# A recurrent attention kernel with a fused SwiGLU block: two more units have their k and r turned by DMAs inside SBUF and VectorE, and the last store is split

## The chip, the cores and the metric

The kernel runs on one core of a Trainium2 chip. The metric is the device time of one execution in microseconds (us), the median of several runs. Lower is better. The engines are named as in the profile: PE is TensorE (PEld its weight loads), DVE is VectorE, ACT is ScalarE, POOL is GpSimd, SP is SyncE, which here only issues DMAs. "SPq" and "ACTq" stand for the DMA issues of SP and ACT.

## What is computed

An RWKV5 attention (4 batches, 8 heads, 768 tokens, head width 48) feeds a SwiGLU feed-forward block with 3072 tokens, model width 384 and inner width 1536. All is float32.

```python
for t in range(S):
    cur = np.einsum('bhd,bhe->bhde', u[None] * kt, vt)
    y[:, :, t] = np.einsum('bhd,bhde->bhe', rt, state + cur)
    state = w[None, :, :, None] * state + np.einsum('bhd,bhe->bhde', kt, vt)
...
g = x @ w_gate
silu = g * (1.0 / (1.0 + np.exp(-g)))
val = x @ w_val
return (silu * val @ w_out).astype(np.float32)
```

## The kernel before

**Units and stages.** The tokens of a batch are cut into six chunks of 128. A unit is one chunk of one batch; there are 24, and unit i is chunk i // 4 of batch i % 4. The function `fast` does the work. (A second function, `general`, only runs when a decay lies outside a range; it does not run here.) The order on every engine is the order of the program text. Units 0 to 3 are written out by hand, then a loop runs over stages s = 4 to 25. Stage s scales k and r of unit s+1 on POOL (`scale`, L299 and L302) and forms its products r·k·u (`own_product`, L228 and L229), loads v of unit s+1 and k and r of unit s+3 (`load_v` L121, `load` L115, both on SP's queue), brings k and r of unit s into transposed form, forms the score matrix of unit s-1 (`scores`, PE at L379, DVE at L384), and computes the outputs of unit s-2 (`outputs`, L409) and its state update (`update`, PE at L424, DVE at L436, POOL at L437).

**Two ways to transpose k and r.** The scaled k and r of the units lie in one tile, `hats`, which has four places for k and two for r. For units below `BLOCKS` (12 before) the function `turn` does 8 PE transposes into two PSUM banks (L341, tile `tp`), and ACT copies both banks to the tiles `kT` and `rT` (L345). From `BLOCKS` on, `move_blocks` issues 16 DMAs on SP's queue (L356, shown as hats<-hats), which arrange 32x32 blocks of one unit's k and r into two spare places of `hats`, and `turn_blocks` has DVE transpose within the blocks, one instruction for `kT` and one for `rT` (L371). The two spare places exist once: `move_blocks` of unit i+1 waits for `turn_blocks` of unit i. In stage s the loop calls `turn_blocks(s)` and then `move_blocks(s + 1)`, behind the scores of unit s-1.

**Places for r.** Below `BLOCKS`, r of unit i lies in place i % 2. From `BLOCKS` on, two consecutive units share a place: `i % 4 // 2`. So units 12 and 13 use one place, 14 and 15 the other. `scale_r` of the second unit of such a pair writes where `move_blocks` of the first reads.

**Feed-forward work.** Groups of 256 tokens (two units) go through gate and value products. `gate_value` (L448) does groups 0 and 1 straight: six matrix products into one of two PSUM banks of the tag `gv`, a sigmoid on ACT (L454), and two products on DVE (L455 and L456) that write `hT`. Later groups, two at a time, go through a scheme with fewer products (`four`, L625). The output projection of two groups is a sequence of items, each of six products into PSUM (`project`, L519). An item "gi" below means item i of the projection, with g the group: 0 or 1 of the pair. The items come in this order:

```python
order = "00 10 01 02 11 04 03 12 05 06 13 14 15 16".split()
```

where the first digit is the group and the second the item. Item 0 of a group takes a bank of the tag `gv` for one of its accumulators; in group 0 that bank is used by item 1. Item 10 and item 01 call `h_sums`, two wide additions each on DVE (L492 to L496), ahead of their matrix products. POOL forms sums of weights (`weight_sum`, L476) that the projections need.

**What fills a stage.** In stages 5 to 11 the table `EARLY` says where a weight is rounded or summed ("R") and where one piece of feed-forward work is fed ("F"). In stages 9 to 11 an F stands behind the scores, another behind outputs and update, and a third at the end of the stage. The piece behind the update in stage 11 is the last gate and value product of group 1; the piece at the stage's end is item 00; items 10, 01 and 02 open the feeding of stage 12.

**The outputs.** ACT issues the DMAs that store the result (L542). For the last pair of groups the tile of the first half of the tokens, `o_sb1`, is filled in two halves by DVE: columns 0 to 191 at item 1 (L529), columns 192 to 383 at item 6 (L533), the last computing instruction of the program. The whole tile is stored after item 6.

Of the kernel before, what the change touches and what calls it, by code (L numbers as in the profile page):

```python
# [15 lines left out]
P = 128  # L16
# [6 lines left out]
def fast(  # L23
# [31 lines left out]
    N = B * NCH  # L55
    DM, DFF = moe_w_gate.shape
# [11 lines left out]
    dve, pool, act, pe, sp = nc.vector, nc.gpsimd, nc.scalar, nc.tensor, nc.sync  # L68
# [26 lines left out]
    khat, rhat = [hats[:, n] for n in (0, 2, 3, 5)], [hats[:, n] for n in (1, 4)]  # L95
# [4 lines left out]
    blocks = [hats[:, n].rearrange("p h x -> p (h x)") for n in (7, 6)]  # L100

    def rhat_of(i):
        return rhat[i % 2 if i < BLOCKS else i % 4 // 2]

    def raw(i):

# [4 lines left out]
    def load(i):  # L111
        c, b = divmod(i, B)
        rows = slice(P * c, P * (c + 1))
        for src, dst in zip((k, r), raw(i)):
            sp.dma_start(out=dst, in_=src[b, :, rows, :].rearrange("h t d -> t h d"))  # L115

    def load_v(i):
        c, b = divmod(i, B)
        rows = slice(P * c, P * (c + 1))
        for e in range(2):  # L120
            sp.dma_start(  # L121
                out=v_ld[i % 4][:, :, 64 * e : 64 * e + D],
                in_=v[b, :, rows, :].rearrange("(a e) t d -> e t a d", e=2)[e],
            )
# [3 lines left out]
    for f in range(FC // 2):  # L128
        for src, dst in ((moe_w_gate, wg), (moe_w_val, wv)):
            cols = slice(2 * P * f, 2 * P * (f + 1))  # L130
# [94 lines left out]
    def own_product(i):  # L225
        kl, rl = raw(i)
        rk = two.tile([P, H, D], FP32, name="rk", tag="rk")[:]
        pool.tensor_mul(rk, rl, kl)  # L228
        pool.tensor_mul(rk, rk, ub[:])  # L229
        rks[i] = rk  # L230

    def own_sum(i):
        dus[i] = three.tile([P, H], FP32, name="du", tag="du")
        dve.tensor_reduce(dus[i][:], rks.pop(i), axis=AX.X, op=ALU.add)
# [9 lines left out]
    for e in range(2):  # L244
# [3 lines left out]
        out=ub[:].rearrange("p h d -> p (h d)"),  # L248
        in_=bass.AP(tensor=u.tensor, offset=u.offset, ap=[[0, P], [1, H * D]]),
# [9 lines left out]
    def warm(n):  # L259
# [9 lines left out]
        out=mask[:], in_=mask[:], compare_op=ALU.is_gt, fill=0.0,  # L269
# [7 lines left out]
    for l in range(7):  # L277
        n = 1 << l
# [15 lines left out]
    def at(i, a):  # L294

        return HP - 1 - a if i >= BLOCKS and i % 2 == 0 else a

# [3 lines left out]
    def scale_r(i):  # L301
        pool.tensor_mul(rhat_of(i)[:, :, 0:D], raw(i)[1], rscale[:])  # L302
# [8 lines left out]
    def scale(i):  # L311
        scale_k(i)
        scale_r(i)
# [18 lines left out]
    def pair(t, a):  # L332
        return t[:, 2 * a : 2 * a + 2, :].rearrange("p e d -> p (e d)")

    def turn(i):
        kr = khat[i % 4], rhat_of(i)
        tps = [ps_a.tile([P, HP, P], FP32, name="tp", tag="a") for _ in kr]
        turned[i] = three.tile([P, HP, P], FP32, name="rT", tag="rT")
        for tp, t, dst, table in zip(tps, kr, (kT[i % 2], turned[i]), (pw[:, :, 1 : P + 1], pv)):
            for a in range(HP):  # L340
                pe.transpose(tp[:, a, :], pair(t, a), ident[:])  # L341
            if i < 4:
                dve.tensor_mul(dst[:], tp[:], table)
            else:
                act.copy(dst[:], tp[:])  # L345
# [21 lines left out]
    def turn_blocks(i):  # L367

        turned[i] = three.tile([P, HP, P], FP32, name="rT", tag="rT")
        for dst, src in ((kT[i % 2], blocks[0]), (turned[i], blocks[1])):  # L370
            dve.transpose(dst[:].rearrange("p a t -> p (a t)"), src)  # L371

    def scores(i):

        ps = [ps_a.tile([P, HP, P], FP32, name="s_ps", tag="a") for _ in range(2)]
        for a in range(HP):
            for e in range(2):
                rows = slice(64 * e, 64 * e + D)
                pe.matmul(  # L379
                    ps[e][:, a, :], kT[i % 2][rows, at(i, a), :], turned[i][rows, at(i, a), :],  # L380
                    start=True, stop=True, skip_group_check=True,
                )
        for e in range(2):
            dve.copy_predicated(  # L384
                At[i % 2][:].rearrange("p (a e) t -> p a e t", e=2)[:, :, e],
                mask[:].bitcast(INT32).unsqueeze(1).to_broadcast([P, HP, P]), ps[e][:],
            )
# [77 lines left out]
    FH, NH = FC // 2, DM // 2  # L465
# [15 lines left out]
    def h_quarters(g):  # L481
        return [
            hT[g][:, FH * k : FH * (k + 1), P * j : P * (j + 1)] for j in range(2) for k in range(2)
        ]
# [13 lines left out]
    def project(g, n):  # L498

        h11, h12, h21, h22 = h_quarters(g)  # L500
        x = part_of.setdefault(g, {})
        if n == 0:
            one_bank = ps_f.tile([P, 2, 2 * P], FP32, name="o_f", tag="gv")[:, 0, 0:NH]
            if g % 2 == 0:
                x["a"] = ps_o.tile([P, 2 * P], FP32, name="o_a", tag="o")[:, 0:NH]
                x["b"] = one_bank
            else:
                x["a"] = one_bank
                x["b"] = ps_w.tile([P, 2 * P], FP32, name="o_b", tag="w_mag")[:, 0:NH]
            x["out"] = [two.tile([P, DM], FP32, name=n, tag=n) for n in ("o_sb1", "o_sb2")]  # L510
        lhs, rhs, acc = (
            (h11, w11, "a"), (h12, w21, "b"), (1, wt[0], "a"), (2, wt[1], "a"),
            (0, w12, "b"), (h22, wt[2], "a"), (3, w22, "b"),
        )[n]
        if isinstance(lhs, int):
            lhs = x["s"][lhs]
        ps = x[acc]
        for f in range(FH):
            pe.matmul(  # L519
                ps, lhs[:, f, :], rhs[:, f, :],  # L520
                start=(f == 0 and n in (0, 1, 4)), stop=(f == FH - 1), skip_group_check=True,
            )
        o1, o2 = x["out"]
        if n in (0, 2, 3):
            nm = {0: "p1", 2: "u2", 3: "u3"}[n]
            x[nm] = six.tile([P, 2 * P], FP32, name=nm, tag="part")[:, 0:NH]
            act.copy(x[nm], ps)
        elif n == 1:
            dve.tensor_add(o1[:, 0:NH], x["p1"], ps)  # L529
        elif n == 5:  # L530
            act.copy(o2[:, 0:NH], ps)
        elif n == 6:
            dve.tensor_add(o1[:, NH:DM], x["u2"], ps)  # L533
        if n in (3, 4):
            if "c22" in x:
                dve.tensor_add(o2[:, NH:DM], x["u3"], x["b"])
            x["c22"] = True
        if n >= 5:
            j = 6 - n
            c, b = divmod(2 * g + j, B)  # L540
            n0 = S * b + P * c
            act.dma_start(out=out[n0 : n0 + P, :], in_=x["out"][j][:])  # L542

# [155 lines left out]
    def gaps(s, n):  # L701

        if s not in EARLY:
            if n == 0:
                share[0] = min(-(-len(todo) // (4 - (s - 9) % 4)), 14)
            feed(share[0] // 5 + (n < share[0] % 5))
            return
        for what in EARLY[s][n]:
            if what == "R":
                if done["pool"] < NW:  # L710
                    round_weights()
                elif len(summed) < 4:
                    weight_sum()
            else:
                feed(1, 3)

    share = [0]
    BLOCKS = 12
    LATE = 12
    EARLY = {s: ("" if s < 7 else "R", "F", "R", "F", "RF") for s in range(5, 12)}  # L720
    EARLY[4] = ("R", "F", "", "F", "F")
# [82 lines left out]
    for s in range(4, N + 2):  # L804
        if 4 < s < N:
            own_sum(s)
        if s + 1 < N:
            scale(s + 1)
            own_product(s + 1)
            load_v(s + 1)  # L810
            if s + 3 < N:
                load(s + 3)
        if s < BLOCKS:
            turn(s)
        gaps(s, 0)
        if 4 <= s - 1 < N:
            while small:
                small.popleft()()
            scores(s - 1)
            if s >= LATE:  # L820
                outputs(s - 2)
                update(s - 2)
            gaps(s, 1)
        if BLOCKS <= s < N:
            turn_blocks(s)
        if BLOCKS <= s + 1 < N:
            move_blocks(s + 1)
        gaps(s, 2)
        if s - 2 >= 4 and (s < LATE or s > N):
            outputs(s - 2)  # L830
            update(s - 2)
        if s >= 5 and s % 2:
            queue((s - 3) // 2)
        if s < N:
            diagonal(s)
        if s - 2 >= 4:
            gaps(s, 3)
        gaps(s, 4)
        if s == 12:

            dve.tensor_tensor(bad[:], held[:], wcol[:], ALU.not_equal)
            dve.tensor_reduce(badc[:], bad[:], axis=AX.X, op=ALU.add)
            dve.memset(ones[:], 1.0)
            n_ps = ps_a.tile([P, HP, P], FP32, name="n_ps", tag="a")
            pe.matmul(n_ps[0:1, 0, 0:1], badc[:], ones[:], start=True, stop=True)
            act.copy(outside, n_ps[0:1, 0, 0:1])
# [417 lines left out]
```

## Time and profile before

| | |
|---|---|
| median of 5 runs | 625.47 us (624.91 to 628.15) |
| the profiled execution | 625.54 us, its span 623.7 us |
| PE busy | 611.1 us, 98% of the span |
| POOL busy | 296.9 us, 48% |
| DVE busy | 359.1 us, 58% |
| ACT busy | 238.8 us, 38% |
| PE transposes, tile tp | 96 of them, the last group at 113.96 us |
| hats<-hats DMAs | 192, from 119.73 us on |
| last computing instruction | DVE L533, 618.30 to 618.65 us |

The trace records one execution. Its span is the time from the first to the last record, and the execution's own time is 1.84 us longer. Busy shares are means over the whole span; PE instructions overlap one another, so the time between two starts says what an instruction costs, and its recorded duration does not.

### The profile page before, as it was taken

To read this page: it belongs to the slowest core of one execution; us is meant where nothing else is said; L and a number is where in the kernel's file an instruction comes from. 1 tells how busy PE (TensorE), PEld (TensorE's weight loads), DVE (VectorE), ACT (ScalarE), POOL (GpSimd) and SP (SyncE) were. 2 spreads that over 40 slices of the span, in tenths; PEclk is the share of its full clock that TensorE was granted. 3 is DMA by queue.
4 is the path that set the end of the run, shared out by engine and by line. 5 is a ranking of instruction groups with operands and counts; after the bars stand their busy time and mean duration, and the time that the engine had idled before them with its cause. 6 is when DMAs were issued, how large, how long until landed. Compare 5 with 4: busy or idle time off the path is not lost.

```text
span 623.7 us, 13014 instructions
## 1 busy us (share of the span) xinstructions
PE 611.1 (98%) x5040; PEld 551.4 (88%) x5040; DVE 359.1 (58%) x751; ACT 238.8 (38%) x647; POOL 296.9 (48%) x350
## 2 busy tenths in 40 slices
PE   8799999999999999999999999999999999999996
PEld 7688888899888899888899888899988899988896
DVE  6878997373566574466575455574354463355460
ACT  3368785322444412344331335422244321233310
POOL 4789789935556315364452636341334211443110
PEclk9999999999999999999999999999999999999999
DMA  7989873233232203323223311221000000000001
GB/s 187 234 201 249 252 249 65 49 64 80 58 61 33 40 15 76 66 42 46 44 34 69 78 16 32 31 42 38 26 1 2 2 0 26 26 1 2 1 2 56
DMA packets 138008, 40.47 MB, mean 65 GB/s; under 512 B 128592, under 2 KB 131792, under 8 KB 137936
## 3 DMA queue, kind: packets, MB, share of 16 engines
q1 hardware_dynamic: 134480, 34.82, 26.1%
q10 hardware_dynamic: 3456, 4.72, 2.1%
q8 instruction: 42, 0.69, 0.4%
q14 instruction: 30, 0.25, 0.1%
HBM read 28.51 MB, written 4.72 MB: 53 GB/s over the span
## 4 chain that ended last, share of the span: by engine, by line
PE 90%; POOL 2%; DMA 1%; ACT 1%; DVE 1%; issue 0%; SPq 0%; ACTq 0%; POOLq 0%
PE c_b L625 25%; PE c_a L625 21%; PE o_f L519 13%; PE o_a L519 8%; PE gv L448 7%; PE o_b L519 6%; PE y_ps L409 5%; PE s_ps L379 3%; PE u_ps L424 1%; PE tp L341 1%; DMA r_ld<-in_r_dram 1%; POOL wg L216 1%; POOL wv L216 1%; POOL rk L228 0%; POOL hats L299 0%
## 5 line engine op out<-in xcount | busy, mean ns | idle before, releaser
L609 POOL TENSOR_TENSOR hT<-hT,u 128x256 f32<-128x256 f32 x60 | 47.0, 785 | 148.7 <-DVE hT L608 121.6
L632 ACT COPY u<-c_a 128x256 f32<-128x256 f32 x120 | 44.5, 371 | 85.7 <-PE c_a L625 83.3
L625 PE MATMUL c_a<-t,wv 128*128 128x256 f32 x240 | 72.0, 382 | 0.1
L625 PE MATMUL c_b<-xT,wg 128*128 128x256 f32 x240 | 71.6, 380 | 0.0
L605 ACT ACTIVATE sg<-hT 128x256 f32<-128x256 f32 x120 | 50.0, 416 | 52.5 <-DVE hT L634 33.8
L320 ACT ACTIVATE At<-ident,du 128x128 f32<-128x128 f32 x176 | 62.0, 398 | 16.0 <-DVE o_sb L533 7.2
L625 PE MATMUL c_b<-xT,s 128*128 128x256 f32 x240 | 61.6, 379 | 0.0
L639 DVE TENSOR_TENSOR u<-u,c_b 128x256 f32<-128x256 f32 x60 | 25.1, 419 | 60.5 <-PE c_b L625 55.3
L625 PEld LDWEIGHTS c_b<-xT,s 128*128 128x128 f32 x240 | 45.2, 190 | 6.6 <-DVE u L639 0.3
L625 PEld LDWEIGHTS c_a<-t,wv 128*128 128x128 f32 x240 | 44.9, 190 | 6.9 <-ACT u L632 1.2
L625 PEld LDWEIGHTS c_b<-xT,wg 128*128 128x128 f32 x240 | 45.3, 190 | 6.0
L634 DVE TENSOR_TENSOR hT<-p,c_b 128x256 f32<-128x256 f32 x60 | 25.2, 420 | 41.4 <-PE c_b L625 38.8
L585 POOL TENSOR_TENSOR s<-wv,wg 128x256 f32<-128x256 f32 x24 | 17.8, 741 | 65.5 <-PE o_f L519 50.8
L384 DVE COPY_PREDICATED At<-mask,s_ps 128x512 f32<-128x512 int32 x48 | 33.0, 741 | 21.4 <-PE s_ps L379 12.5
L302 POOL TENSOR_TENSOR hats<-r_ld,rscale 128x384 f32<-128x384 f32 x20 | 20.8, 1041 | 35.2 <-DMA hats<-hats 25.3
L448 PE MATMUL gv<-xT,wg 128*128 128x256 f32 x144 | 36.7, 391 | 0.6 <-ACT xT L413 0.6
L637 DVE TENSOR_TENSOR hT<-hT,c_a 128x256 f32<-128x256 f32 x60 | 25.3, 421 | 19.4 <-PE c_a L625 18.1
L641 DVE TENSOR_TENSOR hT<-u,c_b 128x256 f32<-128x256 f32 x60 | 25.2, 420 | 19.4 <-PE c_b L625 19.2
L409 PE MATMUL y_ps<-At,v_ld 128*32 128x128 f32 x768 | 34.9, 273 | 1.3 <-issue 1.2
L625 PE MATMUL c_b<-t,s 128*128 128x256 f32 x120 | 36.2, 383 | 0.0
L625 PE MATMUL c_b<-xT,wv 128*128 128x256 f32 x120 | 35.9, 381 | 0.0
L625 PE MATMUL c_a<-t,s 128*128 128x256 f32 x120 | 35.8, 380 | 0.0
(135 smaller groups left out, 1383.9 us busy)
## 6 DMA issues: line engine op xcount, KB each, us to landing
hats<-hats SPq DMA_DIRECT2D x192, 32.0 KB, 2.0
w_bits<-in_moe_w_gate_dram SPq DMA_DIRECT2D x6, 768.0 KB, 6.1
v_ld<-in_v_dram SPq DMA_DIRECT2D x48, 96.0 KB, 3.1
w_bits<-in_moe_w_val_dram SPq DMA_DIRECT2D x6, 768.0 KB, 5.9
w_bits<-in_moe_w_out_dram SPq DMA_DIRECT2D x6, 768.0 KB, 6.4
out_dram<-o_sb ACTq DMA_DIRECT2D x24, 192.0 KB, 1.9
k_ld<-in_k_dram SPq DMA_DIRECT2D x20, 192.0 KB, 2.9
r_ld<-in_r_dram SPq DMA_DIRECT2D x20, 192.0 KB, 3.9
```

The costliest lines, as they stand in the source:

```text
L320: lambda h=h: act.activation(At[i % 2][:, h, :], ident[:], AF.Identity, scale=du[:, h : h + 1])
L384: dve.copy_predicated(At[i % 2][:].rearrange("p (a e) t -> p a e t", e=2)[:, :, e], mask[:].bitcast(INT32).unsqueeze(1).to_broadcast([P, H ...
L409: pe.matmul(ps[32 * q : 32 * q + 32, cc, :], *x, start=start, stop=stop, skip_group_check=True,)
L448: pe.matmul(gv[:, o, :].rearrange("p (i t) -> p i t", i=2), wt[:, c, P * f : P * (f + 1)], xT[:, 2 * g % NX : 2 * g % NX + 2, c, :], start ...
L519: pe.matmul(ps, lhs[:, f, :], rhs[:, f, :], start=(f == 0 and n in (0, 1, 4)), stop=(f == FH - 1), skip_group_check=True,)
L605: act.activation(x[what, f][:], h[j], AF.Sigmoid)
L609: pool.tensor_mul(h[1], h[1], x.pop(("u3", f))[:])
L625: pe.matmul(ps.rearrange("p (i t) -> p i t", i=2), lhs, rhs, start=first, stop=what not in ("p2", "p5", "p4", "p3"), skip_group_check=True,)
L632: act.copy(x[nm, f][:], ps)
L634: dve.tensor_add(h[0], x.pop(("p1", f))[:], ps)
L637: dve.tensor_mul(h[0], h[0], ps)
L641: dve.tensor_add(h[1], x.pop(("u2", f))[:], ps)
```

## The change

`BLOCKS` goes from 12 to 10, so units 10 and 11 leave the path over PE and ACT (`turn`) and take the one over SP's DMAs and DVE (`move_blocks`, `turn_blocks`). The sharing of places for r now starts at unit 8: units 8 and 9 share one place, 10 and 11 the other. `turn(s)` is written ahead of `scale(s + 1)` in the loop, so that the transposes of unit 8 precede the scaling of unit 9 into the same place; on each engine's own list of instructions this alone changes no order. For unit 10 the pairs of heads are now held in reverse order, as they are for other even units from `BLOCKS` on. In the last group the first half of the columns of one output tile is stored as soon as item 1 has filled it, and the store at the end takes the other half alone.

```diff
     def rhat_of(i):
-        return rhat[i % 2 if i < BLOCKS else i % 4 // 2]
+        return rhat[i % 2 if i < 8 else i % 4 // 2]
...
-        if n >= 5:
-            j = 6 - n
+        def store(j, cols):
             c, b = divmod(2 * g + j, B)
             n0 = S * b + P * c
-            act.dma_start(out=out[n0 : n0 + P, :], in_=x["out"][j][:])
+            act.dma_start(out=out[n0 : n0 + P, cols], in_=x["out"][j][:, cols])
+
+        ends = g == N // 2 - 1
+        if n == 1 and ends:
+            store(0, slice(0, NH))
+        elif n >= 5:
+            store(6 - n, slice(NH if n == 6 and ends else 0, DM))
...
-    BLOCKS = 12
+    BLOCKS = 10
...
     for s in range(4, N + 2):
         if 4 < s < N:
             own_sum(s)
+        if s < BLOCKS:
+            turn(s)
         if s + 1 < N:
             scale(s + 1)
             own_product(s + 1)
             load_v(s + 1)
             if s + 3 < N:
                 load(s + 3)
-        if s < BLOCKS:
-            turn(s)
```

## Prediction

> **What bounds the kernel now.** First the page: busy time and the chain that ended last.
>
> ```profile
> PE 611.1 (98%) x5040; PEld 551.4 (88%) x5040; DVE 359.1 (58%) x751; ACT 238.8 (38%) x647; POOL 296.9 (48%) x350
> PE 90%; POOL 2%; DMA 1%; ACT 1%; DVE 1%; issue 0%; SPq 0%; ACTq 0%; POOLq 0%
> ```
>
> PE is the bound, and in stages 9 to 12 it has no gap. What leaves PE there is gained, what makes PE wait there is lost, and no later slack gives either back. So I read the timeline of each engine around stages 9 to 12 (start, duration, engine, line). PE:
>
> ```profile
> 101.81 1.04 PE L341 MATMUL tp<-ident,hats 128*128 128x128 f32 x8
> 102.78 1.16 PE L379 MATMUL s_ps<-rT,kT 48*128 48x128 f32 x16
> ...
> 123.51 2.11 PE L519 MATMUL o_a<-wo,hT 128*128 128x192 f32 x12
> 125.46 4.06 PE L519 MATMUL o_f<-wo,hT 128*128 128x192 f32 x24
> ```
>
> From the start of 8 transposes to the next group: 102.78 - 101.81 = 0.97 us. The last line is items 10 and 01, 1.95 us each. SP, around the first move that exists today (unit 12):
>
> ```profile
> 118.68 0.37 SPq L115 DMA_DIRECT2D k_ld<-in_k_dram  x1
> 119.10 0.57 SPq L115 DMA_DIRECT2D r_ld<-in_r_dram  x1
> 119.73 11.65 SPq L356 DMA_DIRECT2D hats<-hats  x16
> ```
>
> One unit's 16 DMAs hold SP for 11.65 us here, right behind two loads. POOL, stage 10 first, then the scaling of unit 13, which waits for that move:
>
> ```profile
> 102.74 1.01 POOL L299 TENSOR_TENSOR hats<-k_ld,kscale 128x384 f32<-128x384 f32 x1
> 103.70 1.00 POOL L302 TENSOR_TENSOR hats<-r_ld,rscale 128x384 f32<-128x384 f32 x1
> 104.66 1.01 POOL L228 TENSOR_TENSOR rk<-r_ld,k_ld 128x384 f32<-128x384 f32 x1
> ...
> 133.17 1.01 POOL L302 TENSOR_TENSOR hats<-r_ld,rscale 128x384 f32<-128x384 f32 x1 [8.72 <-DMA hats<-hats]
> ```
>
> The move that began at 119.73 lets its waiter go at 133.17: 13.44 us. DVE, stage 11 into 12, and today's first block transpose:
>
> ```profile
> 119.78 0.42 DVE L456 TENSOR_TENSOR hT<-sg,gv 128x256 f32<-128x256 f32 x1
> 120.98 0.74 DVE L436 TENSOR_TENSOR Z<-u_ps,Z 48x192 f32<-48x192 f32 x2 [0.78 <-PE u_ps L424]
> 124.13 0.42 DVE L455 TENSOR_TENSOR sg<-sg,gv 128x256 f32<-128x256 f32 x1 [2.40 <-ACT sg L454]
> 124.58 0.42 DVE L456 TENSOR_TENSOR hT<-sg,gv 128x256 f32<-128x256 f32 x1
> ...
> 141.39 0.71 DVE L371 STREAM_TRANSPOSE kT<-hats 128x512 f32<-128x512 f32 x1
> 142.03 0.67 DVE L371 STREAM_TRANSPOSE rT<-hats 128x512 f32<-128x512 f32 x1
> 142.62 0.38 DVE L567 TENSOR_TENSOR t<-xT 128x256 f32<-128x256 f32 x1
> ```
>
> In the new order the transposes of unit 11 stand between the first L456 and L436 here.
>
> **What it removes.** 16 PE transposes, two groups of 8, at 0.97 us each: -1.94 us on the bound. Four ACT copies (two of 0.57 and two of 0.59 us in these rows) go too; ACT is 38% busy and idle for up to 2.6 us before its sigmoids there, so they are worth nothing. The new place of `turn` in the text changes no engine's order; scaling unit 9 now needs unit 8's transposes, which began at 77.52 and took about 1 us, and its r scaling starts at 79.86. Nothing.
>
> **What it adds.** Two moves (32 DMAs on SP) and four DVE transposes of 0.67 to 0.71 us. These transposes stand in DVE's fixed order, so the question is when each move lands.
>
> Move of unit 10. In stage 9 SP has issued the loads of unit 12 at 94.47 + 0.57 = 95.04, and scaling unit 10 ended at 93.05, so the move starts at 95.10. It stands behind the same two loads as today's first move, so I take 13.44: landed at 108.54. Behind it on SP wait the loads of v of unit 11, needed two stages later, and of k and r of unit 13. Two waiters: DVE comes to the transposes of unit 10 when its L456 ends, 108.05 today, 107.08 with one PE group gone; it waits 1.46 us, is done with both at +1.23 (142.62 - 141.39), then does L436, and is free at 110.5, before its next product at about 111.0. No cost. POOL wants to scale r of unit 11 into the shared place at 103.70, and now waits until 108.54: 4.84 us, and behind it queue the products of unit 11, three weight sums and unit 12. The sum that item 02 needs ended at 115.78 today, so 120.6; item 02 starts at 129.36 today. That wait is hidden on PE.
>
> Move of unit 11. It needs unit 11 scaled, but also stands on SP behind the loads of unit 13, which wait for the first product of unit 11 on POOL. From 108.54: +0.96 to that product (104.66 - 103.70), +1.04 until SP issues the load (105.69 against 104.66), +1.05 for both loads (119.73 - 118.68). The move starts at 111.59 and lands, 13.44 later, at 125.03.
>
> DVE comes to the transposes of unit 11 at 120.20 - 1.94 = 118.26 and stands still until 125.03, 6.8 us. Behind it are L436, then L455 and L456 of the last gate and value product. L456 ends at 125.03 + 1.23 + 0.77 (L436) + 0.87 (124.13 to 125.00) = 127.90. That L456 frees the PSUM bank into which item 10 accumulates. PE would come to item 10 at 125.46 - 1.94 = 123.52; today the bank is free at 125.00, only 0.46 us ahead. So PE waits 127.90 - 123.52 = 4.38 us. Item 02 needs L493 of the sums, some 2.3 us behind L456 (125.00 to 127.33), and comes 3.9 us behind item 10: no second wait. Unit 12's move then starts about 126.4 and lands by 139.9, while DVE asks for it at 141.39 plus the shift: covered. If that cover failed, each further microsecond would be PE's.
>
> The split store. The last DMA of 192 KB moves most of its bytes between 619.5 and 620.5; with half the bytes at most about 0.4 us go, and nothing if the landing (1.9 us for 192 KB stores, 2.0 us for 32 KB moves) is all fixed. I take -0.2. The early half costs an ACT issue of 0.34 us in a queue that idles 1.6 us and more between its copies there: nothing, or 0.3 if it delays one.
>
> Sum: -1.94 + 4.38 - 0.2 = +2.24 us. 625.54 + 2.24 = 627.8 us; the profiled execution lies 0.07 above the median, which I neglect.
>
> **Bounds.** The trace does not show a move in stage 9 or 10. The quickest that it shows with a waiter started at 166.12 and let POOL go at 177.99: 11.87 us, far from any load. Both moves that quick: 106.97, then 110.02, then 121.89, L456 ends at 124.76, PE waits 1.24, the sum is -0.9: 624.6 us. I take 13.44 for both since each follows two loads within 0.1 us, as that one did. A transfer still slower than 13.44 is possible, since v of unit 11 now crosses SP ahead of unit 13's loads: up to 1 us more.
>
> PE then idles over 4 us in one piece, which it does nowhere in the middle of this trace (longest there 1.2 us). The only row for it is at the end, after the last matmul at 618.28, in the windows view (clock is the third number from the right end):
>
> ```profile
> core 0: us, PE busy (x) PEld busy (x) DVE busy (x) ACT busy (x) POOL busy (x), PEclk, DMA share, GB/s
> 622.50:623.00 0.50, 0.00 (x0) 0.00 (x0) 0.00 (x0) 0.00 (x0) 0.00 (x0) 0.91 0.00 0
> 623.00:623.50 0.50, 0.00 (x0) 0.00 (x0) 0.00 (x0) 0.00 (x0) 0.00 (x0) 0.50 0.10 33
> ```
>
> The clock falls to half some 4.6 us after PE stops. At 4.4 us it may or may not fall; if it stays half for as long as it took to fall, PE loses 2.3 us: 630.1. I count that at one in four.
>
> The Trainium skill, "TensorE: Matmul & The Clock Gate", Part 1, says that a free-running window of about 3.4 us decides, so an idle of 4.4 us covers a whole window only for some phases, and that a cold PE needs another such window to recover. By it the loss would be, as an estimate, 1.7 us, and the sum 629.5 us. The trace's one row agrees with a fall after one full window.
>
> The skill's "DMA: Bandwidth & Descriptors", Rules for kernel authors, speaks against this path as a whole: transfers under 64 KB pay mostly overhead, and these have 32 KB. With its fixed cost of about 2 us paid 16 times in a row, a move would last some 33 us by estimate and the time would rise by tens of microseconds. The trace shows that the issues overlap, 0.65 us apart, so I go by the trace.
>
> **Rivals.**
> 1. *The moves are quick or overlap better; the stall eats the gain.* Both near 12 to 12.5 us: net -0.9 to +0.8, 624.6 to 626.3. For it: most moves hold SP only 10.4 us. Against: those did not follow loads.
> 2. *DVE's wait stays off PE; the 16 transposes are gained whole.* 625.54 - 1.94 - 0.2 = 623.4 us. It holds if unit 11's move lands by 125.03 - 4.38 = 120.65. From 95.10 that leaves 25.55 us for two moves and 3.05 us between them, so 11.25 us per move; the quickest seen is 11.87. It also comes out if PE has other work ahead of item 10, and its order has none.
> 3. *The stall with the half clock:* 629.5 to 630.5.
> 4. *The change does not do what it says*, for instance transposes left on PE. The listed order of the new kernel has none for units 10 and 11, so I give it nothing.
>
> **Chances.** My forecast, a stall of about 4 us with the clock held, 0.48 (627.0 to 628.6); half clock 0.17; rival 1 0.27; rival 2 0.08. About 0.3% is what a measurement of this kernel can tell from no change: 1.9 us. Faster (below 623.6): rival 2, 0.08. Slower (above 627.4): the half clock and most of my forecast, 0.17 + 0.45 = 0.62. Within: the rest, 0.30. The range leaves out rival 2 and the upper end of the half clock: 624.6 to 629.9.
>
> **What would show it.** Right: no tp group in stages 10 and 11; DVE waits about 6.8 us for hats<-hats ahead of L371 near 118 to 125; POOL's L302 waits near 104 to 108; PE idles about 4.4 us ahead of o_f at L519, with DVE's L456 as releaser; move 10 starts at 95.1 and move 11 at 111.6. Wrong: PE passes from item 00 to item 10 without a gap, a move lands in under 11.3 us, or a PE gap opens elsewhere, for instance at item 02 or the scores of unit 12. The DVE wait with an early enough landing would give rival 2; a granted clock under 1 near 128 to 135 gives rival 3.

## The result, and the profile after

The changed kernel takes 626.16 us (median; 624.63 to 628.51), the kernel before, with all its runs taken together, 625.47 us. The ratio of the means is 1.0013, with a 95% interval of 1.0008 to 1.0018: slower by about 0.8 us, and so within the 0.3% that the prediction counted as no change (a chance of 0.30, against 0.62 for slower). I predicted 627.8 us, in a range of 624.6 to 629.9. The time came out in the range, but below what I called my forecast (627.0 to 628.6, 0.48): it lies in the range of my first rival ("the stall eats the gain", 624.6 to 626.3, 0.27). The profiled execution took 626.01 us, its span is 624.3 us.

The page of the changed kernel, busy time and the chain that ended last:

```profile
PE 610.5 (98%) x5024; PEld 549.6 (88%) x5024; DVE 361.1 (58%) x755; ACT 236.8 (38%) x643; POOL 298.7 (48%) x350
PE 87%; SPq 3%; DMA 3%; DVE 2%; ACT 2%; POOL 2%; issue 1%; DVEq 0%; ACTq 0%; POOLq 0%
```

16 products and 16 weight loads have gone from PE, and PE is busy 0.6 us less. But the chain runs over PE for 87% instead of 90% of the span; 6% instead of 1% now lie with SP's issues and with DMAs. The chain passes over SP in two places: near 111 to 122 us, which is the move of unit 11, and near 281 to 292 us, which is the move of unit 18. The first place comes first. "Move 11" stands for the 16 DMAs of unit 11, and so on. SP, the two new moves (start, duration):

```profile
94.49 11.45 SPq L356 DMA_DIRECT2D hats<-hats  x16
...
110.13 0.57 SPq L115 DMA_DIRECT2D r_ld<-in_r_dram  x1
110.80 11.41 SPq L356 DMA_DIRECT2D hats<-hats  x16
```

POOL and DVE wait for them, and then DVE works off what stood behind its wait:

```profile
107.72 1.00 POOL L302 TENSOR_TENSOR hats<-r_ld,rscale 128x384 f32<-128x384 f32 x1 [4.26 <-DMA hats<-hats]
...
123.60 0.71 DVE L371 STREAM_TRANSPOSE kT<-hats 128x512 f32<-128x512 f32 x1 [5.40 <-DMA hats<-hats]
...
126.02 0.42 DVE L456 TENSOR_TENSOR hT<-sg,gv 128x256 f32<-128x256 f32 x1
126.82 0.95 DVE L492 TENSOR_TENSOR hs<-hT 128x768 f32<-128x768 f32 x1
127.80 1.15 DVE L493 TENSOR_TENSOR hs<-hs,hT 128x768 f32<-128x768 f32 x1
```

And PE, items 00, 10, 01 and 02 of the projection, in this order:

```profile
121.52 2.11 PE L519 MATMUL o_a<-wo,hT 128*128 128x192 f32 x12
123.47 2.11 PE L519 MATMUL o_f<-wo,hT 128*128 128x192 f32 x12
126.58 2.19 PE L519 MATMUL o_f<-wo,hT 128*128 128x192 f32 x12 [1.00 <-DVE hT L456]
129.10 2.19 PE L519 MATMUL o_a<-wt,hs 128*128 128x192 f32 x12 [0.32 <-DVE hs L493]
```

An item costs 1.95 us from start to start. Item 10 begins without a wait. Item 01 should begin at 123.47 + 1.95 = 125.42 and begins at 126.58, 0.14 us behind the end of L456: 1.16 us lost. Item 02 should begin at 128.53 and begins at 129.10: another 0.57 us.

To see where the rest went, I followed one mark through the traces, PE's first score product (L379) of each stage, and took its time minus that in the kernel before. The change of this difference along the kernel, in us, for the profiled execution of every kernel (minus is gain; "start" is the difference at stage 9, ahead of which nothing relevant was changed except in e6 to e10 and e12, where products were put in or taken out at the start; the starts of executions scatter from -0.3 to +1.4; the next four columns end at the marks of stages 11, 12, 15 and 19):

| kernel | start | stages 10, 11 | stage 12 | stages 13 to 15 | stages 16 to 18 | later | behind L533 | span against before |
|---|---|---|---|---|---|---|---|---|
| after | -0.25 | -1.75 | +1.81 | +0.40 | +0.59 | -0.01 | -0.23 | +0.56 |
| e1 store split only | 0.65 | 0 | 0 | 0.01 | -0.01 | -0.01 | -0.10 | 0.54 |
| e2 without store split | 0.93 | -1.75 | 2.01 | -0.07 | 0.64 | 0 | 0.02 | 1.78 |
| e3 unit 11 only | 1.07 | -0.88 | 0.01 | 0.13 | 0.50 | 0 | -0.14 | 0.69 |
| e4 turn unit 11 later | 0.14 | -1.75 | 2.29 | 0.41 | 0.57 | 0 | -0.27 | 1.39 |
| e5 load behind move 11 | 0.51 | -1.75 | 2.29 | -0.07 | 0.72 | 0.01 | 0.11 | 1.82 |
| e6 filling products | 0.15 | -1.75 | 2.57 | -0.07 | -0.01 | 0.01 | -0.13 | 0.77 |
| e7 both | 0.65 | -1.75 | 1.46 | -0.06 | -0.02 | 0 | -0.18 | 0.10 |
| e8 before, fewer warm-ups | 0.92 | 0 | 0 | 0 | 0.60 | -0.01 | 0.03 | 1.54 |
| e9 unit 11 only, filled | 0.16 | -0.88 | 0 | 0.03 | 0.33 | -0.01 | -0.15 | -0.52 |
| e10 e7, four sums early | -0.09 | -1.75 | 4.87 | 0.46 | -0.02 | 0 | -0.27 | 3.20 |
| e11 four sums early | 1.35 | -1.75 | 4.72 | 0.41 | 0.56 | -0.01 | -0.26 | 5.02 |
| e12 e7, two sums early | 0.34 | -1.74 | 0.50 | 0.42 | -0.01 | -0.01 | -0.15 | -0.65 |

The row "after" says it: 1.75 us come from the transposes, stage 12 takes 1.81 back, and a further 1.0 us is lost in two places that the prediction did not name, near 191 and 302 us. Each row is one execution. Stage 12 has the same order in "after", e2 and e6 and loses 1.81, 2.01 and 2.57 us there, so differences of up to 0.8 us in this column can be chance.

### The profile page after: what moved, and what is told of

Same layout as the page of the kernel before. It is cut to its first block, busy times and chain, and to the rows that moved or that the text cites. A ratio compares the mean times of both kernels' runs of the same rounds, so it can differ in the third digit from the quotient of the medians.

```text
span 624.3 us, 13021 instructions
## 1 busy us (share of the span) xinstructions
PE 610.5 (98%) x5024; PEld 549.6 (88%) x5024; DVE 361.1 (58%) x755; ACT 236.8 (38%) x643; POOL 298.7 (48%) x350
## 3 DMA queue, kind: packets, MB, share of 16 engines
q10 hardware_dynamic: 3600, 4.72, 2.1%
HBM read 28.51 MB, written 4.72 MB: 53 GB/s over the span
## 4 chain that ended last, share of the span: by engine, by line
PE 87%; SPq 3%; DMA 3%; DVE 2%; ACT 2%; POOL 2%; issue 1%; DVEq 0%; ACTq 0%; POOLq 0%
PE c_b L630 23%; PE c_a L630 19%; PE o_f L519 12%; PE o_a L519 7%; PE gv L448 7%; PE o_b L519 6%; PE y_ps L409 5%; PE s_ps L379 3%; SPq L356 3%; PE warm L263 1%; DMA w_bits<-in_moe_w_val_dram 1%; DMA hats<-in_r_dram 1%; PE u_ps L424 1%; PE tp L341 1%; DMA hats<-hats 1%
## 5 line engine op out<-in xcount | busy, mean ns | idle before, releaser
L637 ACT COPY u<-c_a 128x256 f32<-128x256 f32 x120 | 44.5, 371 | 84.1 <-PE c_a L630 83.1
L639 DVE TENSOR_TENSOR hT<-p,c_b 128x256 f32<-128x256 f32 x60 | 25.2, 420 | 42.3 <-PE c_b L630 39.3
L302 POOL TENSOR_TENSOR hats<-r_ld,rscale 128x384 f32<-128x384 f32 x20 | 20.8, 1040 | 37.8 <-DMA hats<-hats 37.8
```

Source lines behind the costliest of these rows:

```text
L637: act.copy(x[nm, f][:], ps)
L639: dve.tensor_add(h[0], x.pop(("p1", f))[:], ps)
```

## Experiments

### The parts alone: e1, e2, e3

e1 is the kernel before with the store split and nothing else. e2 is the change without the split. e3 turns only unit 11 in the new way. Every ratio below is to the runs of the kernel before in the same batch. Their median was 625.39 us for e1 to e4, 626.07 for e5 to e8, 625.47 for e9 to e11 and 626.29 for e12, so times of different batches can't be set side by side.

```diff
# e2
-        ends = g == N // 2 - 1
+        ends = False
# e3
-    BLOCKS = 10
+    BLOCKS = 11
```

> The kernel before with the split store alone (units 10 and 11 stay on PE). Theory: the end after the last computing instruction shrinks by about 0.2 us (before: 5.05 us from the end of L533 to the end of the span; with the whole change 4.86), so 625.3 us. Rival: the landing is fixed and the 0.2 us is chance; 625.5 us and an end of 5.05 us.

> The change without the split store. Theory: PE gains 1.75 us from the 16 transposes and gives back 1.7 us at items 01 and 02 of the projection, and loses 0.5 to 1 us later; with the long store at the end, 626.4 us, and PE waits 1.0 us or more for L456. Rival (the later losses were chance of one execution): 625.5 us.

> BLOCKS = 11: unit 10 is turned on PE again, unit 11 alone moves. Theory: unit 11's move no longer follows unit 10's; it starts near 106.7 and lands near 120, DVE waits at most 1 us for it and PE does not wait for L456. 8 transposes are gained, 0.88 us, and 0.2 us of store: 624.4 us. Rival (whatever makes unit 11 late lies in its own stage, not in two moves in a row): DVE waits 3 us or more and the time is 625.5 us or above.

e1: 625.18 us, ratio to before 0.9993 (0.9981 to 1.0005). e2: 627.28 us, 1.0027 (1.0015 to 1.0040). e3: 625.21 us, 0.9995 (0.9985 to 1.0005).

The time of e1 can't be told from no change. Of the eleven profiles with the split, ten show 0.10 to 0.27 us less behind L533 and e5 0.11 us more; e2 and e8, without it, show 0.02 and 0.03 us more. So the split is worth some 0.1 to 0.25 us. e2 is 0.9 us slower than I expected; in its profile 0.93 us lie ahead of stage 9, where nothing differs from the kernel before. In e3 DVE comes to the transposes of unit 11 0.47 us before the move has landed and loses nothing on PE: one unit's 0.88 us is kept whole in stage 12. Only the second unit brings the stall, because its move can begin only when the first one's is over and DVE has turned it (move 11 starts at 107.77 in e3 and at 110.80 in the changed kernel). In e3, too, half a microsecond is lost in stages 16 to 18, where nothing was changed.

### The wait moved: e4

DVE's turn of unit 11, and with it the move of unit 12, stands behind the last gate and value product of stage 11.

```diff
-        if BLOCKS <= s < N:
+        if BLOCKS <= s < N and s != 11:
             turn_blocks(s)
-        if BLOCKS <= s + 1 < N:
+        if BLOCKS <= s + 1 < N and s != 11:
             move_blocks(s + 1)
...
             gaps(s, 3)
+        if s == 11:
+            turn_blocks(s)
+            move_blocks(s + 1)
         gaps(s, 4)
```

> The change, with the block transposes of unit 11 (and the move of unit 12 behind them) placed behind the last gate and value product instead of ahead of the state update: DVE does L436, L455 and L456 first. Theory: L456 no longer stands behind the DMA wait, items 01 and 02 start without a gap, and the 1.7 us come back: 624.4 us, or 623.6 if the later losses go as well. Rival (PE loses for another reason, such as wide additions or weight sums being late): PE waits at item 02 instead, 626 us.

626.25 us, 1.0006 (0.9991 to 1.0020). L456 no longer stands behind the move, and item 01 follows item 10 without a gap. The wait has gone to the next item. PE in e4:

```profile
123.86 4.06 PE L519 MATMUL o_f<-wo,hT 128*128 128x192 f32 x24
129.97 2.19 PE L519 MATMUL o_a<-wt,hs 128*128 128x192 f32 x12 [2.05 <-DVE hs L493]
```

Item 02 waits 2.05 us for the wide sum L493, which DVE now reaches late. Stage 12 loses 2.29 us, no less than the 1.81 to 2.57 of the kernels with the old order. So the bank of L456 is not the whole stall: whatever DVE does behind the move is late by as much, and L493 is next in line.

### The later losses: e5 to e8

Two theories were open for the 0.6 us near 302: a move that runs into loads, or a fetch of instructions that falls into a move. The trace's list of DMA packets has, beside the kernel's transfers, fetches of instructions: one queue brings 16 KB at a time, about one fetch for every 240 of PE's products and weight loads together (42 in the span of the kernel before, 41 in the changed one), another 8 KB at a time. That the first is PE's is shown by e8 below, where PE's stream alone is shorter and these fetches move. PE's fetch at 280.0 us in the kernel before starts just ahead of move 18 (281.15); in the changed kernel, with 32 fewer instructions on PE, it comes at 286.6, in the middle of it. SP, move 18, and POOL's scaling of unit 19, which waits for it, first the kernel before, then the changed one, there with PE's wait behind it:

```profile
281.15 10.42 SPq L356 DMA_DIRECT2D hats<-hats  x16
...
293.36 1.00 POOL L302 TENSOR_TENSOR hats<-r_ld,rscale 128x384 f32<-128x384 f32 x1 [6.88 <-DMA hats<-hats]
```
```profile
281.34 11.47 SPq L356 DMA_DIRECT2D hats<-hats  x16
...
294.60 1.00 POOL L302 TENSOR_TENSOR hats<-r_ld,rscale 128x384 f32<-128x384 f32 x1 [7.93 <-DMA hats<-hats]
...
302.42 0.70 PE L630 MATMUL c_a<-t,wv 128*128 128x256 f32 x2 [0.34 <-ACT p L637]
```

POOL's scaling started at 293.36 before and at 294.60 now, and the DVE and ACT work of the following pieces shifts until PE waits for ACT (L637, 0.3 us by the view of waits, 0.6 us by the mark).

e5 issues the load of unit 13's rows behind move 11. e6 puts eight one-column products into the start of the kernel, which brings PE's instruction count back to 5040. e7 does both. e8 is the kernel before with eight warm-up products fewer: nothing of the change, but PE's stream is shorter by the same 32 instructions.

```diff
# e5
-            if s + 3 < N:
+            if s + 3 < N and s != 10:
                 load(s + 3)
...
             move_blocks(s + 1)
+        if s == 10:
+            load(s + 3)
# e6
             pe.matmul(ps[:, 0, :], ident[:], ident[:], start=True, stop=True)
+        return ps
...
-    warm(2)
+    ps = warm(2)
+    for _ in range(8):
+        pe.matmul(ps[0:1, 1, 0:1], ident[:, 0:1], ident[:, 0:1], start=True, stop=True)
# e8, on the kernel before
-    warm(18)
+    warm(10)
```

> The change, with the loads of k and r of unit 13 issued behind unit 11's move instead of ahead of it. Theory: the move starts when unit 11 is scaled and unit 10's block transposes are done, near 109 instead of 110.8, lands near 121.2 instead of 123.6, L456 ends ahead of item 01, and the 1.8 us that PE gave back in stage 12 stay gained: against the change as it is -1.8 us, 624.4 us. Rival (the order of the loads does not matter, the DMAs are slow by themselves): it lands near 123.6, 626.2 us.

> The change, with 8 one-column matrix products added early, where PE idles, so that PE's stream of instructions is from stage 11 on as long as in the kernel before (16 weight loads and 16 products against the removed 16 and 16). They compute nothing that is used. Theory (the later losses come from instruction fetches of PE, 16 KB each, that now fall into a move on which POOL waits): the fetch near 286 goes back to near 280, the move of unit 18 holds SP for 10.4 us instead of 11.5, POOL scales unit 19 a microsecond earlier, PE does not lose 0.6 us near 302: 625.5 us. Rival (the later losses come from POOL and DVE getting in each other's way after the late stage 12): unchanged, 626.2 us.

> Both of the former: loads of unit 13 behind unit 11's move, and PE's stream filled up. Theory: 16 transposes gained (-1.75 us), the store (-0.2), no loss in stage 12, none near 302, perhaps 0.4 near 190: 623.5 to 623.9 us, faster than both kernels. Rival: as without the fill.

> The kernel before with 10 instead of 18 products in its warm-up, which nothing uses: PE's stream is shorter by 16 weight loads and 16 products, as in the change, and nothing else differs. Theory (fetches): the fetch near 280 moves into the move of unit 18 (281 to 292), which holds SP for about 11.4 us, and PE loses 0.5 us near 302: 626.0 us. Rival: the same time as before, 625.5 us, and the move at 10.4 us. Should the clock be lower in the first microseconds because of the shorter warm-up, that shows ahead of 60 us and is left out.

e5: 627.15 us, 1.0022 (1.0008 to 1.0036). e6: 626.72 us, 1.0023 (1.0006 to 1.0041). e7: 625.95 us, 1.0002 (0.9988 to 1.0016). e8: 627.16 us, 1.0018 (1.0005 to 1.0032).

The column "stages 16 to 18" decides for the fetch. All four kernels with the full filling (e6, e7, e10, e12) lose nothing there (-0.02 to -0.01), all with the change and without filling lose 0.56 to 0.72, and e8, which has none of the change, loses 0.60. Move 18 in e6, then in e8:

```profile
282.05 10.42 SPq L357 DMA_DIRECT2D hats<-hats  x16
```
```profile
282.07 11.51 SPq L356 DMA_DIRECT2D hats<-hats  x16
```

The fetch lies at 280.9 in e6 and at 287.2 in e8. The filling did not make the whole faster: in e6 stage 12 happened to lose 2.57 us, since the second move reached DVE at 124.74.

The load (e5, e7) did less than I expected. DVE and SP in e5:

```profile
110.20 0.67 DVE L371 STREAM_TRANSPOSE rT<-hats 128x512 f32<-128x512 f32 x1
```
```profile
110.93 11.70 SPq L356 DMA_DIRECT2D hats<-hats  x16
```

Move 11 began at 110.93, 0.06 us behind DVE's turn of unit 10, which empties the two spare places; in the changed kernel it began 1.78 us behind that turn (109.02 and 110.80). But in e5 move 10 itself landed late, 13.38 us after its start instead of 12.84, so that against the stage only 0.6 us are left of this. In e7 it is 1.5 us. Item 01 lost less, item 02 more. PE in e7, where item 01 follows without a gap and item 02 waits:

```profile
124.36 4.20 PE L520 MATMUL o_f<-wo,hT 128*128 128x192 f32 x24
129.65 2.19 PE L520 MATMUL o_a<-wt,hs 128*128 128x192 f32 x12 [1.09 <-DVE hs L494]
```

(In e6, e7, e9, e10 and e12 the line numbers are higher by one.)

### One unit, filled: e9

e3 with four of the filling products.

> Unit 11 alone turned by VectorE and DMAs, output in two halves, and four one-column products put in so that TensorE's instruction stream keeps its old length (four products in place of... the sixteen instructions that the move took away come partly back). Theory (the step of 0.5 us near stage 18 comes from an instruction fetch that has moved into a chain of DMAs): the gain of 0.87 for eight transposes stays to the end of the span, 0.1 to 0.2 more at the store, 0.1 paid for the products: 624.4 to 624.7, no step near 302. Rival (the step has to do with the turning itself): as without the products, 625.2, with the step of 0.5 at stage 18.

625.03 us, 0.9986 (0.9973 to 1.0000). It has the lowest ratio of all kernels here, 0.4 us under before by the medians, and its interval just reaches 1. The 0.88 us are gained, and move 18 is back at 10.40 us. The column of stages 16 to 18 shows 0.33, not 0: this loss comes near 317 us, one move later, and e3 has it too: of its 0.50 us, 0.33 come there and 0.17 near 302 us, where e9 loses nothing. So the filling undid what lies near 302; the cause of the loss near 317 stays open.

### DVE's sums ahead of its wait: e10, e11, e12

What is left in stage 12 of e7 is the wait of item 02 for the wide sums. DVE stands idle for over 4 us ahead of the second move, and the data of these sums are there by then. e11 puts all four sums of group 0 ahead of the turn of unit 11 in the changed kernel, e10 does the same in e7, and e12, made after the result of these two, puts only the two sums there that item 02 needs.

```diff
# e10, e11 (e12: h_sums(0, 0) alone)
+        if s == 11:
+            h_sums(0, 0)
+            h_sums(0, 1)
         if BLOCKS <= s < N:
             turn_blocks(s)
...
             if (j, p) in ((1, 0), (0, 1)):
-                h_sums(g, p)
+                if g > 0:
+                    h_sums(g, p)
```

> The change, the load of unit 13's rows behind move 11, eight one-column products that keep TensorE's instruction stream at its old length, and in stage 11 the wide sums of group 0 put ahead of VectorE's turn of unit 11, so that VectorE does them while it waits for the move. Theory (what is left in stage 12 is VectorE's work behind the move: item 02 waits for its sums): stage 12 no longer loses 1.46 but 0 to 0.3, nothing lost at stage 18; 1.75 of transposes and 0.2 of the store are kept: 623.6 to 624.2, faster than both. Rival (the wait goes elsewhere, to the bank of item 01 or to the moves): 625.5 to 626.

> The change with only one thing else: the wide sums of group 0 ahead of VectorE's turn of unit 11 in stage 11. Theory: item 02's wait for its sums (0.57) goes, item 01's wait for the bank (1.16) stays or shrinks a little, the step near stage 18 stays: 625.4 to 625.8. Rival (the wait for the move sets all, whatever order VectorE has): 626.2, as the change.

e10: 628.81 us, 1.0044 (1.0024 to 1.0063). e11: 629.38 us, 1.0055 (1.0036 to 1.0074). Both are the reverse of what I expected. DVE and POOL in e10:

```profile
121.23 1.26 DVE L496 TENSOR_TENSOR hs<-hT 128x768 f32<-128x768 f32 x1
122.41 3.38 DVE L497 TENSOR_TENSOR hs<-hT,hs 128x768 f32<-128x768 f32 x1
125.72 0.70 DVE L372 STREAM_TRANSPOSE kT<-hats 128x512 f32<-128x512 f32 x1
```
```profile
121.75 3.23 POOL L477 TENSOR_TENSOR wt<-wo 128x1152 f32<-128x1152 f32 x1
124.93 1.72 POOL L300 TENSOR_TENSOR hats<-k_ld,kscale 128x384 f32<-128x384 f32 x1
```

One addition of 128x768, which takes 0.95 us at its quickest here (L492 in the changed kernel), took 3.38 us here, and ended 0.81 us behind POOL's weight sum. The four took from 118.28 to 125.79, 7.5 us, where I had reckoned with the 4 to 5 us that were free. The turn of unit 11 no longer waits for the move but for DVE: the move had landed at 124.51, and the turn began at 125.72. In e11 these are 125.03 and 127.08. All behind it is later by that. In e10 something else adds to it: move 10 landed only 15.13 us after its start (12.84 in the changed kernel), so move 11 began late as well. e11, where move 11 landed within 0.2 us of the changed kernel's against the stage, is the clean case.

That POOL is what slows such an addition is seen in all fourteen traces together. They hold 672 additions of this size; the 381 beside which POOL does nothing took 0.91 to 0.96 us each, and the 288 that run beside POOL for over 0.3 us took 0.95 to 3.38 us, half of them over 1.36.

PE's wait grows to 3 us, and this is where the clock falls. PE in e11, then the windows view of e11 (the clock is the third number from the right end):

```profile
125.07 2.12 PE L519 MATMUL o_f<-wo,hT 128*128 128x192 f32 x12
130.05 3.80 PE L519 MATMUL o_f<-wo,hT 128*128 128x192 f32 x12 [2.87 <-DVE hT L456]
133.69 2.11 PE L519 MATMUL o_a<-wt,hs 128*128 128x192 f32 x12
```
```profile
129.50:129.75 0.25, 0.00 (x0) 0.00 (x0) 0.25 (x1) 0.00 (x0) 0.25 (x1) 1.00 0.25 45
129.75:130.00 0.25, 0.00 (x0) 0.00 (x0) 0.25 (x2) 0.00 (x0) 0.25 (x1) 0.84 0.58 91
130.00:130.25 0.25, 0.20 (x1) 0.23 (x2) 0.25 (x1) 0.00 (x0) 0.25 (x1) 0.50 0.00 0
...
133.00:133.25 0.25, 0.25 (x2) 0.25 (x2) 0.00 (x0) 0.00 (x0) 0.00 (x0) 0.50 0.78 102
133.25:133.50 0.25, 0.25 (x3) 0.25 (x2) 0.00 (x0) 0.00 (x0) 0.00 (x0) 0.83 0.04 6
```

PE begins item 01 3.03 us late (130.05 against 125.07 + 1.95) and then needs 133.69 - 130.05 = 3.64 instead of 1.95 us for it, at half clock: 3.03 + 1.69 = 4.72 us, the whole loss of stage 12 in the table. e10 shows the same: 3.11 us late, and the item itself 3.59 us.

> The change, the load of unit 13's rows behind move 11, the eight one-column products, and only the first two wide sums of group 0 (those that item 02 needs) ahead of VectorE's turn of unit 11. Theory (four sums, slowed beside GpSimd to 7.4 us in all, did not fit into the 4 to 5 us for which VectorE waits for the move, two of about 3 us do): VectorE is free when the move lands, item 01 does not wait, item 02 no longer waits for its sums (1.09 in the kernel with the load behind the move and the products), so stage 12 loses about 0.4 instead of 1.46, and the time is 1.1 below that kernel's: 624.6 to 625.1. Rival (any sum put there delays GpSimd's scaling or the turn, and the wait for item 01's bank comes back, past 2.5 us with the clock at half behind it): 626 to 629.

e12: 625.17 us, 0.9996 (0.9979 to 1.0014). PE in e12:

```profile
124.06 2.11 PE L520 MATMUL o_f<-wo,hT 128*128 128x192 f32 x12
126.44 2.19 PE L520 MATMUL o_f<-wo,hT 128*128 128x192 f32 x12 [0.27 <-POOL rk L229]
128.47 2.11 PE L520 MATMUL o_a<-wt,hs 128*128 128x192 f32 x12
```

Two sums fit, but only just: they took 3.15 and 1.64 us instead of about 3 together, and DVE came to the turn of unit 11 at 123.47, when the move had landed at 122.96. Item 02 waits for nothing, item 01 waits 0.43 us, where I had expected no wait, and stage 12 loses 0.50 instead of 1.46 us, close to the 0.4 that I expected. (The view names POOL as releaser of item 01; item 01 begins 0.14 us behind the end of DVE's second product for `hT` here too, as in all these kernels where it waits.) Its profiled execution took 624.89 us, with a span 0.65 us under that of before. But its runs scatter from 624.13 to 629.19 us. By the medians it is 1.1 us under the kernel before of its batch, by the means 0.3, and the interval allows no verdict: no version is shown to beat both kernels.

## Why the prediction was right or wrong

**Right: what is removed.** No product of tile tp is left in stages 10 and 11, and they are shorter by 0.88 and 0.87 us: 1.75, where I had 1.94. Eight transposes alone take 0.97 us from start to start, but in the sequence 0.88 goes with them.

**Right: the shape of the stall.** Move 10 started at 94.49 (predicted 95.10) and let its waiters go after 13.23 us (13.44). POOL waited 4.26 us at L302 (4.84). Move 11 started at 110.80 (111.59) behind the loads of unit 13, and reached DVE after 12.80 us. DVE waited 5.40 us (6.8), and L456 ended at 126.44 (127.90). Each of these terms was too large by some tenths, in all 1.5 us at the end of L456. The loads were, as I had put it, the last thing that held move 11 back; in e5 and e7, with the loads out of the way, it is the spare places, which DVE's turn of unit 10 empties. The length of the moves, though, came out for a reason that the runs speak against: I took 13.44 because two loads stand ahead of each, and in e5 and e7 move 11 has them behind it and still holds SP for 11.70 and 11.58 us. What goes with the length is the instruction fetch, as the last section shows.

**Wrong: "That L456 frees the PSUM bank into which item 10 accumulates."** It is item 01's bank. Item 10 started 2.97 us ahead of the end of L456. PE thus had one item more to do, 1.95 us of cover. Since L456 was also earlier, the wait was 1.16 us instead of 4.38. By the code, items 10 and 01 both accumulate into a bank of the tag `gv`; I took the busy one to be item 10's without checking which is which. In every kernel here in which item 01 waits, it begins 0.14 to 0.15 us behind the end of this L456.

**Wrong: "no second wait."** With the true order, item 02 follows 1.95 us behind item 01, not 3.9 us behind the first wait, and L493 was not done: 0.57 us. I had also taken the sums at the durations of a trace where POOL did other things at that time. e4 shows that this wait is the next to decide once L456 is out of the way. Had item 10 been the waiter, as I wrote, PE would have lost about 3 us there. Two of the signs that I had named for being wrong came: PE passed from item 00 to item 10 without a gap, and a gap opened at item 02.

**Not in the sum: 1.0 us of later losses.** "Four ACT copies ... worth nothing", "changes no order": I looked for what the change moves on the engines and not for what it moves in their instruction streams. The 0.6 us near 302 is the fetch, shown by e6, e7, e8, e10 and e12. The 0.4 us near 191 is seen in five kernels and missing in others; there a product of DVE (L613) took 0.89 us in the changed kernel instead of 0.43 before, while POOL formed weight sums, and then PE waited for L639. Filling does not decide it (e10 and e12 have it, e2 and e5 don't), and what does is open.

**Right: the split store**, -0.2: 5.06 us from the end of L533 to the end of the span before, 4.83 after.

So, in the prediction's own terms: -1.75 + 1.16 + 0.57 + 0.40 + 0.59 - 0.2 = +0.8 us in place of +2.24, and the medians differ by 0.7. The time is that of the first rival, but only in part for its reason: it needed moves of 12 to 12.5 us, and they took 13.2 and 12.8. (By my own sum such moves give -0.6 to +0.4 us, and not the -0.9 to +0.8 that I wrote beside this rival.) The range held because it took in this rival, which is luck where the forecast is concerned. The short wait came from the other bank, and the second wait and the later losses took what that left.

**The half clock** did not come, since PE's longest idle piece in stage 12 was 1 us. For the stall that I forecast, one in four was too low a chance: in the profiled executions of e10 and e11 the clock fell with idle pieces of 2.9 us.

## What to carry to other kernels

When a step frees a buffer, follow in the program which later piece really takes that buffer: one item of work more or less was 1.95 us here, more than the 1.75 us that the transposes gave. An engine's idle time ahead of a wait is only free for work that fits into it at the speed that it has there: four sums that took 3.7 us in the kernel before took 7.5 us beside POOL. And when two kernels differ in an untouched place, look at the instruction fetches: taking instructions away shifts all later ones, and a filling of a few empty products tells this from other causes.

## What the hardware did that I had not expected

- **Instruction fetches delay chains of small DMAs.** A chain of 16 DMAs of 32 KB holds SP for 10.4 us when undisturbed (10.42 in the kernel before and in e6) and for 11.5 us when one 16 KB fetch for PE falls into it (11.47 after, 11.51 in e8). The fetches in the trace at 98.3 and 119.2 us fall into both new moves, which held SP for 11.45 and 11.41; so these moves, and the first of the kernel before (11.65, a fetch at 120.9), may be slow for this reason and not for the loads ahead of them, as I had put it. The fourteen traces have 188 such chains. The 87 without any instruction fetch hold SP for 10.40 to 10.48 us, but for one of 10.75; the 65 into which a fetch for PE falls more than 1 us ahead of their end hold it for 10.64 to 12.13, half of them for over 11.4. So a chain with such a fetch is 0.2 to 1.7 us longer, and what decides how much is open.
- **DVE and POOL hold each other up by more than I had reckoned with.** The Trainium skill, "SBUF — State Buffer", Terms, says that the two share a pair of ports as an exclusive lock, held for the whole instruction, and that the loser blocks. L497 in e10 (3.38 us, ending 0.81 us behind POOL's instruction) agrees with it. But most additions beside POOL take less, 1.36 us in the middle instead of 0.95, and POOL's own scaling took 1.72 instead of 1.00 us: here mostly each of the two is slowed in part.
- **The clock falls earlier than the end of the trace suggested.** There it fell some 4.6 us behind the last product; in e11 it fell about 2.7 us behind the modelled end of the last product before the gap (127.19), and stayed at half for 3.4 us (129.9 to 133.3). In e10 it fell 0.4 us after PE had already begun again (129.1 against 128.69), and stayed there for 3.4 us. The skill's "TensorE: Matmul & The Clock Gate", Part 1, gives a window of about 3.4 us that runs freely, and half clock after at least one idle window. The time at half clock agrees with the window, but idle pieces of 2.87 us (e11) and 2.95 us (e10), less than a window, were enough; the 2.05 us of e4 were not.
